# Eight zero writes and four weight loads around the start of the first mixture of experts: two of the writes and all four loads change their place

## The chip, the cores and the metric

The kernel runs on one core of a Trainium2 chip. The metric is the device time of one launch in microseconds (us), as the median of several runs. Below, PE is the matrix engine, DVE the vector engine, ACT the scalar engine, POOL the GpSimd engine and SP the engine that issues most DMAs. POOL also issues DMAs: all indirect ones (gathers and scatters) and some plain ones.

## The reference, cut to what matters

Attention over chunks with a few memory keys gives 1536 rows `x` of 512 numbers. Two mixtures of experts follow, each with 8 experts of two matrices (512x1024 and 1024x512). In the first, every row goes to its two best experts, in the second to its best one as far as the expert has room.

```python
x = attn_out.transpose(0, 2, 1, 3).reshape(B * S, H * D)          # 1536 x 512
# first mixture: for each expert e and each of the two choices k
h = np.maximum(x[mask] @ w1[e], 0.0)
out[mask] += top2_w[mask, k, None] * (h @ w2[e])
# second mixture: the same with the best expert alone and a capacity of 384 rows
```

## The kernel before, in words

**Stages.** The attention runs in 12 steps `t`, one for each tile of 128 rows. `step(t)` works at several tiles at once: scores of tile t+2, `prob` of t+1, `attend` and `normalise` of t (which write the tile `xs`), the transposes of t-1 (`x_tr`, L315) and the gate logits of t-2 (L325, copied by DVE at L326). Routing work for the first four tiles (`route`, L518 on) is fed into DVE's queue between these from step 5 on. Each engine runs its instructions in the order in which the code issues them.

**Rows in DRAM.** `put_x` (L309) writes each tile `xs` to DRAM. There are four buffers for `xs`, so tile t may be written only when the row block of tile t-4 has landed. All puts are issued by SP, in one queue with everything else that SP issues.

**Zeros.** The first mixture adds its results into a DRAM array with an accumulating scatter, so the array must be zero first. It is filled by eight plain DMAs of 520 KB from an SBUF tile `zero` (`blank_rows`, L1388). The table `ZEROS` says how many of them SP issues in which step of the attention; the rest are issued by POOL later, by `meanwhile`.

**Jobs of the first mixture.** Rows are gathered by expert and run as jobs. The first job `V0` takes up to 128 rows of expert 0 from the first four tiles and runs in full precision. The second job, `V8`, is the full job of expert 0: 312 rows, gathered by POOL in three blocks (L775, `ids_l`). PE transposes each block (L783); before the third it runs three filler matmuls (L231, `HEAT`). Then V8's matmuls follow (L835). The other seven experts are ranked by their number of rows and run as S[0] to S[6]; their weights can be loaded only when the ranking is known.

**Weights.** A weight matrix comes in halves of 512 KB (`half`, loads at L749, issued by SP). `raw(h)` loads half h; 8 to 11 are the first four halves of the first ranked expert. ACT and DVE split each into two parts (L769, L770), and a buffer is free again when its half has been split. Halves 8 and 9 use buffers that are free from the start; 10 and 11 must wait for V8's own halves. With `behind`, POOL first writes one element of the buffer, so that the load must wait for what stands ahead in POOL's queue.

**Scatter.** After V0's last matmul its rows are added to the zeroed array by a scatter (L1012), which POOL issues and which waits for all eight zero writes. The gathers of S[0] stand behind it in POOL's queue.

Of the kernel before, what the change touches and what calls it, by code (L numbers as in the profile page):

```python
# [42 lines left out]
RB = 6  # L43
PACE = (1.1, 1.9)
PIECES = {6: (2, 3), 7: (0,), 8: (1,), 9: (4,), 10: (5,)}
ZEROS = {0: 1, 1: 2, 3: 1}
HEAT = (0, 0, 3)
ZT = 2
ZN = 2
# [8 lines left out]
def attention_two_moe_kernel(  # L58
# [7 lines left out]
    nc = tc.nc  # L66
# [120 lines left out]
    xb, st = {}, {}  # L187
# [445 lines left out]
    def ranks(cnt, nv, tag, keep=None):  # L633

        key = rt.tile([128, nv], F32, name="key" + tag)
        nc.vector.scalar_tensor_tensor(key, cnt, 16.0, rev[:, 0:nv], op0=OP.mult, op1=OP.add)
        yield "d"
        if keep is not None:
            nc.vector.tensor_tensor(key, key, keep, op=OP.mult)
            yield "d"  # L640
        cmp_ = rt.tile([128, nv, nv], F32, name="cmp" + tag)
        sq = [128, nv, nv]
        nc.vector.tensor_tensor(cmp_, key[:, None, :].to_broadcast(sq), key[:, :, None].to_broadcast(sq),
                                op=OP.is_gt)
        yield "d"
        rk = rt.tile([128, nv], F32, name="rk" + tag)
        nc.vector.tensor_reduce(rk, cmp_, axis=AX.X, op=OP.add)
        yield "d"
        sel = rt.tile(sq, F32, name="sel" + tag)
        nc.vector.tensor_tensor(sel, iotE[:, 0:nv, None].to_broadcast(sq), rk[:, None, :].to_broadcast(sq),  # L650
                                op=OP.is_equal)
        yield "d"
        od = rt.tile(sq, F32, name="od" + tag)
        nc.vector.tensor_tensor(od, sel, iotE[:, None, 0:nv].to_broadcast(sq), op=OP.mult)
        yield "d"
        odi = rt.tile([128, nv], I32, name="odi" + tag)
        with nc.allow_low_precision(reason="whole numbers"):
            nc.vector.tensor_reduce(odi, od, axis=AX.X, op=OP.add)
        regs = [reg_of(odi[0:1, s:s + 1], nv - 1) for s in range(nv)]
        return sel, lambda s: regs[s]()  # L660
# [25 lines left out]
    def out_ids(ids, raw, sh, pl, tag):  # L686

        t = pl.tile(sh, F32, name="oid" + tag)
        nc.vector.tensor_scalar(t, raw, 0.0, float(2 * N), op0=OP.is_equal, op1=OP.mult)
        o = pl.tile(sh, I32, name="oids" + tag)  # L690
        nc.vector.scalar_tensor_tensor(o, t, float(-NP), ids, op0=OP.add, op1=OP.add)
        return o
# [43 lines left out]
    def half(n, j, wa, wb, r, i, behind=False):  # L736

        h = 2 * n + j
        tag = "A" if h % 4 < 2 else "B"
        raw = wp[tag].tile([128, 2, 512], F32, name="raww", bufs=2)  # L740
        sl = ds(r, 1) if not isinstance(r, int) else slice(r, r + 1)
        if i < 2:
            src = wa[sl].rearrange("e (k p) f -> p (e k) f", p=128)[:, 2 * j:2 * j + 2, 512 * i:512 * i + 512]
        else:
            f = 4 * (i - 2) + 2 * j
            src = wb[sl].rearrange("e (k p) f -> p (e k) f", p=128)[:, f:f + 2, :]
        if behind:
            nc.gpsimd.memset(raw[0:1, 0, 0:1], 0.0)
        nc.sync.dma_start(raw, src)  # L749
        st["half", h] = raw  # L750
# [71 lines left out]
    def run_until(done):  # L822

        while not done():
            bg["next"] = bg["credit"]
            tick(0.0)
# [560 lines left out]
    def blank_rows(z, n, w, eng=nc.sync):  # L1387
        eng.dma_start(z, zero[:, None, 0:w].to_broadcast([128, n, w]))  # L1388
# [19 lines left out]
    V0 = Job("T", 0, caps1[0], True, cols=0)  # L1408
# [4 lines left out]
    n = 0  # L1413
# [54 lines left out]
    zeros = [(zr[:, ZN * i:ZN * i + ZN], ZN, W2) for i in range((N + NP) // (128 * ZN))]  # L1468
    zeros2 = [(zo[:, 4 * i:4 * i + 4], 4, DM) for i in range(N // 512)]
    for t in range(-2, NT):  # L1470
# [4 lines left out]
        if t == ZT:  # L1475
            blank_rows(x_d[0:NP].rearrange("(t p) c -> p t c", p=128), 4, W1)
        for _ in range(ZEROS.get(t, 0)):
            blank_rows(*zeros.pop())
# [44 lines left out]
    def raw(h, behind=False):  # L1523
        n, j = divmod(h, 2)
        s, i = divmod(n + 2 if n >= nh + 2 else n, 4)
        if s < E:
            half(n, j, w1a, w2a, st["regs1"](s - 1) + 1, i)
        elif s == E:
            run_until(lambda: "reg_u" in st)
            half(n, j, w1b, w2b, st["reg_u"](), i)  # L1530
        elif s < 2 * E:
            half(n, j, w1b, w2b, st["regs2"](ORDER2[s - E - 1]), i, behind)


    def h_rank():
        st["sel1"], st["regs1"] = yield from ranks(cnt1[:, 1:E], E - 1, "1")
        for h in range(8, 12):
            raw(h)

    def h_ids():  # L1540
        sel = st["sel1"]
# [30 lines left out]
    def chain():  # L1572
        assert not state["gen"]
        logits(NT - 1)
        yield "lg"
        yield from last
        yield from h_rank()
        yield "ranked"
        for i in range(len(BT)):
            yield from enter(i)  # L1580
        yield "d"
        h_open()
        yield from h_ids()
        yield "z"
        yield from h_rest()
# [197 lines left out]
    def hook(job, u, f):  # L1783
        hooks.setdefault((at[job], u), []).append(f)
# [17 lines left out]
    V0.turns = [2.5, 3, 3]  # L1802

    def meanwhile():
        while zeros:
            blank_rows(*zeros.pop(), nc.gpsimd)
        while next(bg["gen"]) != "ranked":
            pass
        bg["next"] = bg["ready"] = bg["credit"]

    hook(V0, 1.5, meanwhile)
    assert S[4].kind == "M" and S[5].kind == "M"
    S[4].late = overflow_done
    U0.late = drain
# [15 lines left out]
    for job in jobs[1:-1]:  # L1830
        n = job.n0
# [69 lines left out]
```

## Time and profile before

| | |
|---|---|
| time, median of 3 runs | 613.57 us (613.55 to 613.66) |
| profiled execution | 613.34 us, of which 611.6 us from the first to the last instruction |
| PE busy | 587.5 us (96%) |
| DVE, ACT, POOL busy | 371.2 us (61%), 300.0 us (49%), 169.4 us (28%) |
| granted PE clock, mean | 0.99 |
| DMA | 112.12 MB, 183 GB/s over the span |

PE is busy nearly all the time, so what can move the total is PE's idle time and the stretches in which its clock is granted at half. A row of the timeline gives start, duration, engine, line, operation, the tile written and the tiles read, and in brackets the idle time of the engine before it and what ended that. Rows of neighbouring equal instructions are merged (x4). The clock is 1.00 at 2.4 GHz and 0.50 at 1.2 GHz. DMA share is the mean busy share of the core's DMA engines.

### The profile page before, as it was taken

To read this page: it belongs to the slowest core of one execution; us is meant where nothing else is said; L and a number is where in the kernel's file an instruction comes from. 1 tells how busy PE (TensorE), PEld (TensorE's weight loads), DVE (VectorE), ACT (ScalarE), POOL (GpSimd) and SP (SyncE) were. 2 spreads that over 40 slices of the span, in tenths; PEclk is the share of its full clock that TensorE was granted. 3 is DMA by queue.
4 is the path that set the end of the run, shared out by engine and by line. 5 is a ranking of instruction groups with operands and counts; after the bars stand their busy time and mean duration, and the time that the engine had idled before them with its cause. 6 is when DMAs were issued, how large, how long until landed. Compare 5 with 4: busy or idle time off the path is not lost. (4 is left out here: it accounts for less than half of the span.)

```text
span 611.6 us, 12271 instructions
## 1 busy us (share of the span) xinstructions
PE 587.5 (96%) x4539; PEld 522.4 (85%) x4539; DVE 371.2 (61%) x997; ACT 300.0 (49%) x633; POOL 169.4 (28%) x243
## 2 busy tenths in 40 slices
PE   7789999899999999999999999999999999999996
PEld 4678774788999999999999898998978978869984
DVE  8575857577755555555555447364468657457672
ACT  4365444335644445445445445344417557456563
POOL 8885004102612312214112140202351121210202
PEclk9899899899999999999999999999999999999999
DMA  9977863536864855756536665545365676975751
GB/s 245 289 131 268 279 190 81 185 87 207 236 230 139 223 161 142 224 156 141 177 90 150 174 143 156 125 125 156 39 206 177 234 238 203 394 274 178 250 187 41
DMA packets 76426, 112.12 MB, mean 183 GB/s; under 512 B 28225, under 2 KB 28225, under 8 KB 76360
## 3 DMA queue, kind: packets, MB, share of 16 engines
q1 hardware_dynamic: 66936, 86.86, 45.1%
q0 software_dynamic: 9424, 24.41, 16.9%
q8 instruction: 38, 0.62, 0.4%
q14 instruction: 28, 0.23, 0.1%
HBM read 88.90 MB, written 22.07 MB: 181 GB/s over the span
## 5 line engine op out<-in xcount | busy, mean ns | idle before, releaser
L770 DVE TENSOR_TENSOR wlo<-raww,whi 128x512 fp32r<-128x512 f32 x226 | 150.2, 688 | 38.5 <-ACT whi L769 32.3
L769 ACT ACTIVATE whi<-raww 128x512 fp32r<-128x512 f32 x228 | 135.6, 623 | 5.3 <-SPq L1340 2.1
L847 DVE SCALAR_TENSOR_TENSOR hl<-psA,hh 128x256 fp32r<-128x256 f32 (+7 forms) x104 | 53.3, 513 | 76.1 <-ACT hh L846 72.4
L846 ACT ACTIVATE hh<-psA 128x256 fp32r<-128x256 f32 (+7 forms) x104 | 47.3, 455 | 100.7 <-PE psA L835 93.3
L835 PE MATMUL psA<-xh,wlo 128*128 128x256 f32 (+7 forms) x416 | 85.5, 327 | 1.8 <-issue 0.7
L835 PE MATMUL psA<-xl,whi 128*128 128x256 f32 (+7 forms) x416 | 82.6, 321 | 0.0
L835 PE MATMUL psA<-xh,whi 128*128 128x256 f32 (+7 forms) x416 | 82.6, 321 | 0.0
L1012 POOL DMA_INDIRECT x_rows<-yr,ids x25 | 39.2, 1569 | 124.7 <-ACT whi L769 85.6
L835 PEld LDWEIGHTS psA<-xh,wlo 128*128 128x128 f32 x416 | 66.9, 190 | 4.1 <-DVE hl L847 0.8
L835 PEld LDWEIGHTS psA<-xl,whi 128*128 128x128 f32 x416 | 68.8, 190 | 0.4
L835 PEld LDWEIGHTS psA<-xh,whi 128*128 128x128 f32 x416 | 68.6, 189 | 0.3
L775 POOL DMA_INDIRECT xg<-x_rows,ids x37 | 37.9, 1025 | 109.0 <-DVE gs L1052 37.6
L835 PE MATMUL psC<-wlo,hh 128*128 128x512 f32 (+1 forms) x184 | 52.6, 405 | 0.0
L835 PE MATMUL psC<-whi,hh 128*128 128x512 f32 (+1 forms) x184 | 50.7, 395 | 0.0
L835 PE MATMUL psC<-whi,hl 128*128 128x512 f32 (+1 forms) x184 | 50.5, 394 | 0.0
L787 DVE TENSOR_TENSOR xl<-psB,xh 128x512 fp32r<-128x512 f32 (+4 forms) x33 | 21.1, 640 | 38.1 <-ACT xh L786 35.2
L835 PEld LDWEIGHTS psC<-whi,hh 128*128 128x128 f32 (+1 forms) x184 | 34.0, 186 | 8.3
L835 PEld LDWEIGHTS psC<-whi,hl 128*128 128x128 f32 (+1 forms) x184 | 34.1, 186 | 8.0
L835 PE MATMUL psA<-hh,wlo 128*128 128x312 f32 (+4 forms) x160 | 36.9, 351 | 0.8 <-DVE hl L847 0.5
L786 ACT ACTIVATE xh<-psB 128x512 fp32r<-128x512 f32 (+4 forms) x33 | 18.4, 557 | 38.8 <-PE psB L783 36.2
L835 PEld LDWEIGHTS psC<-wlo,hh 128*128 128x128 f32 (+1 forms) x184 | 32.0, 186 | 5.4
L1019 POOL DMA_INDIRECT out_dram<-yr,oids x12 | 12.0, 1002 | 87.8 <-ACT yr L990 49.2
(366 smaller groups left out, 933.8 us busy)
## 6 DMA issues: line engine op xcount, KB each, us to landing
raww<-in_moe_w_dram SPq DMA_DIRECT2D x114, 512.0 KB
raw<-in_k_dram SPq DMA_DIRECT2D x6, 512.0 KB
raw<-in_q_dram SPq DMA_DIRECT2D x6, 512.0 KB
x_rows<-xs SPq DMA_DIRECT2D x12, 256.0 KB
out_dram<-zero SPq DMA_DIRECT2D x3, 1024.0 KB
v<-in_v_dram SPq DMA_DIRECT2D x10, 256.0 KB
x_rows<-zero SPq DMA_DIRECT2D x4, 520.0 KB
x_rows<-zero POOLq DMA_DIRECT2D x4, 520.0 KB
```

The lines of the kernel that those rows point to most:

```text
L769: nc.scalar.activation(hi[:, c], raw, AF.Copy)
L770: (eng or nc.vector).tensor_tensor(lo[:, c], raw, hi[:, c], op=OP.subtract)
L775: return nc.gpsimd.indirect_dma_start(out=xg, out_offset=None, in_=src, in_offset=bass.IndirectOffsetOnAxis(ap=ids_ap, axis=0))
L786: nc.scalar.activation(xh[:, :, o], pv[:, :, 0:n], AF.Copy)
L787: low = lambda: nc.vector.tensor_tensor(xl[:, :, o], pv[:, :, 0:n], xh[:, :, o], op=OP.subtract)
L835: nc.tensor.matmul(ps, w[a], x[b], start=first and i == 0, stop=last and i == n - 1)
L846: nc.scalar.activation(hh[:, f, 0:C], ps[:, 0:C], AF.Relu)
L847: nc.vector.scalar_tensor_tensor(hl[:, f, 0:C], ps[:, 0:C], 0.0, hh[:, f, 0:C], op0=OP.max, op1=OP.subtract)
L1012: wr = nc.gpsimd.indirect_dma_start(out=x2_d, out_offset=off, in_=yr[:n], in_offset=None, compute_op=OP.add)
L1019: wr = nc.gpsimd.indirect_dma_start(out=out, out_offset=off, in_=yr[:n, 0:DM], in_offset=None, bounds_check=N - 1, oob_is_err=False)
```

## The change

The table `ZEROS` loses two writes: SP issues one in step 0 and one in step 1, where it issued one, two, and one more in step 3. The remaining six go to POOL, where four were. `h_rank` no longer issues the loads of halves 8 to 11. A new hook, `weights8`, at the end of V0, issues the zero writes and then the four loads, halves 8 and 9 with `behind`.

```diff
-ZEROS = {0: 1, 1: 2, 3: 1}
+ZEROS = {0: 1, 1: 1}
...
-            half(n, j, w1a, w2a, st["regs1"](s - 1) + 1, i)
+            half(n, j, w1a, w2a, st["regs1"](s - 1) + 1, i, behind)
...
         st["sel1"], st["regs1"] = yield from ranks(cnt1[:, 1:E], E - 1, "1")
-        for h in range(8, 12):
-            raw(h)
...
     def meanwhile():
-        while zeros:
-            blank_rows(*zeros.pop(), nc.gpsimd)
         while next(bg["gen"]) != "ranked":
             pass
...
+    def weights8():
+        while zeros:
+            blank_rows(*zeros.pop(), nc.gpsimd)
+        for h in range(8, 12):
+            raw(h, h < 10)
+
     hook(V0, 1.5, meanwhile)
+    hook(V0, 3, weights8)
```

The order on PE, DVE and ACT stays the same. On POOL, before, from the routing results of the last eight tiles (`gt`) to the gathers of S[0] (`ids_2201`):

```order
L515 TENSOR_TENSOR gt<-gt 128x72
L775 DMA xg<-x_rows,ids_l 128x521 x3
L1388 DMA x_rows<-zero 128x2x520 x4
L1010 MEMSET spacer 1x1
L1012 DMA x_rows<-yr,ids_e 2048x520
L775 DMA xg<-x_rows,ids_2201 128x521 x4
```

The same place in the changed kernel:

```order
L515 TENSOR_TENSOR gt<-gt 128x72
L775 DMA xg<-x_rows,ids_l 128x521 x3
L1388 DMA x_rows<-zero 128x2x520 x6
L748 MEMSET raww 1x1 x2
L1010 MEMSET spacer 1x1
L1012 DMA x_rows<-yr,ids_e 2048x520
L775 DMA xg<-x_rows,ids_2203 128x521 x4
```

The zero writes stood behind V8's three gathers already; there are two more of them, and the two one-element writes that halves 8 and 9 wait for stand behind them.

On SP, before, in the attention from step 0 to step 4 (`memv` rows are small copies of memory values, the 128x4x521 write is another zero fill, of the rows array):

```order
L1388 DMA x_rows<-zero 128x2x520
L309 DMA x_rows<-xs 128x512
L141 DMA v_76<-memv 8x2x520 x2
L1388 DMA x_rows<-zero 128x2x520 x2
L309 DMA x_rows<-xs 128x512
L141 DMA v_76<-memv 8x2x520 x2
L1388 DMA x_rows<-zero 128x4x521
L309 DMA x_rows<-xs 128x512
L141 DMA v_76<-memv 8x2x520 x2
L1388 DMA x_rows<-zero 128x2x520
L309 DMA x_rows<-xs 128x512
```

The same stretch in the changed kernel:

```order
L1388 DMA x_rows<-zero 128x2x520
L309 DMA x_rows<-xs 128x512
L141 DMA v_76<-memv 8x2x520 x2
L1388 DMA x_rows<-zero 128x2x520
L309 DMA x_rows<-xs 128x512
L141 DMA v_76<-memv 8x2x520 x2
L1388 DMA x_rows<-zero 128x4x521
L309 DMA x_rows<-xs 128x512
L141 DMA v_76<-memv 8x2x520 x2
L309 DMA x_rows<-xs 128x512
```

One zero write fewer stands ahead of the second, third and fourth put, and the one just ahead of the fourth put is gone too.

On SP, before, the loads of the first halves of the ranked expert, with what each waits for (`DMAHW` is the landing of an earlier DMA of SP's):

```order
L668 TENSOR_LOAD odi_1870 [waits DVE_49]
L668 ISA x2
L749 ISA
L749 DMA raww<-in_moe_w_dram 128x2x512 [waits DMAHW7_49]
L749 ISA
L749 DMA raww<-in_moe_w_dram 128x2x512 [waits DMAHW0_49]
```

The same loads in the changed kernel:

```order
L668 TENSOR_LOAD odi_1864 [waits DVE_49]
L668 ISA x2
L749 ISA
L749 DMA raww<-in_moe_w_dram 128x2x512 [waits DMAHW5_49,Pool_49]
L749 ISA
L749 DMA raww<-in_moe_w_dram 128x2x512 [waits DMAHW6_49,Pool_49]
```

Both loads now wait for POOL; nothing else on SP has changed its order there.

## Rows read from the trace of the kernel before

**Rows 1.** PE's waits, 86 to 250 us: waiting, for whom, total us, times, longest
```profile
PE psD L783 <- DMA xg<-x_rows,ids_l: 2.8, 1, 2.8
```

**Rows 2.** PE's waits, 250 to 612 us
```profile
PE psB L783 <- DMA xg<-x_rows,ids_ul: 1.0, 1, 1.0
```

**Rows 3.** PE's timeline, around the start of V8
```profile
103.31 0.60 PE L783 MATMUL psD<-ident,xg 128*128 128x128 f32 x4
...
105.91 0.81 PE L231 MATMUL psD<-warmer 128*128 128x512 bf16 x3
109.49 0.63 PE L783 MATMUL psD<-ident,xg 128*128 128x128 f32 x4 [2.77 <-DMA xg<-x_rows,ids_l]
110.56 0.95 PE L835 MATMUL psA<-xh,wlo 128*128 128x312 f32 x4 [0.45 <-ACT xh L786]
```

**Rows 4.** POOL's timeline, the same place and on
```profile
99.65 1.21 POOL L775 DMA_INDIRECT xg<-x_rows,ids_l  x1 [3.89 <-DVE wlo L770]
...
102.42 0.95 POOL L775 DMA_INDIRECT xg<-x_rows,ids_l  x1 [0.30 <-issue]
103.37 2.95 POOL L1388 DMA_DIRECT2D x_rows<-zero  x4
...
119.78 1.70 POOL L1012 DMA_INDIRECT x_rows<-yr,ids_e  x1 [13.39 <-DVE yr L1006]
135.95 1.39 POOL L775 DMA_INDIRECT xg<-x_rows,ids  x1 [14.47 <-issue]
```

**Rows 5.** SP's timeline, 101 to 104 us
```profile
102.31 1.03 SPq L749 DMA_DIRECT2D raww<-in_moe_w_dram  x2
```

**Rows 6.** Half-us windows: stretch, length, PE busy, granted clock, DMA share, GB/s
```profile
105.50:106.00 0.50, 0.50 (x6) 1.00 0.65 94
...
109.00:109.50 0.50, 0.01 (x1) 1.00 1.03 419
...
111.00:111.50 0.50, 0.50 (x4) 0.63 1.06 399
...
114.50:115.00 0.50, 0.50 (x5) 0.95 0.28 83
```

**Rows 7.** DVE's timeline in the attention
```profile
57.66 0.42 DVE L303 TENSOR_TENSOR xs<-psC,rs 128x256 f32<-128x256 f32 x1 [2.30 <-DMA x_rows<-xs]
...
66.11 0.17 DVE L326 COPY lgs<-psD 128x18 f32<-128x18 f32 x1
```

**Rows 8.** SP's timeline in the attention
```profile
49.92 0.97 SPq L1388 DMA_DIRECT2D x_rows<-zero  x2
51.01 0.98 SPq L309 DMA_DIRECT2D x_rows<-xs  x1
```

**Rows 9.** Windows: stretch, length, DVE busy, granted clock, DMA share, GB/s
```profile
52.00:54.00 2.00, 1.03 (x3) 1.00 1.01 372
...
57.66:66.28 8.62, 8.17 (x42) 1.00 0.86 261
```

**Rows 10.** PE's timeline in the attention
```profile
58.30 1.36 PE L288 MATMUL psC<-v,ex 64*32 64x65 f32 x64 [0.20 <-PE psB L272]
...
62.81 1.11 PE L288 MATMUL psC<-v,ex 64*32 64x65 f32 x64
...
66.33 0.18 PE L554 MATMUL psD<-msk,tri 128*128 128x36 bf16 x1 [1.02 <-DVE lgs L326]
```

**Rows 11.** Half-us windows in the attention, columns as in group 6
```profile
66.50:67.00 0.50, 0.50 (x16) 0.76 0.29 20
...
70.00:70.50 0.50, 0.50 (x5) 0.83 1.06 402
```

**Rows 12.** A half-us window at another short idle time, columns as in group 6
```profile
48.00:48.50 0.50, 0.15 (x4) 1.00 1.02 391
```

**Rows 13.** ACT's timeline: a weight split in the attention, the first use of half 8
```profile
69.32 0.63 ACT L769 ACTIVATE whi<-wlo 128x512 fp32r<-128x512 f32 x1 [1.92 <-DMA wlo<-in_moe_w_dram]
...
134.46 1.14 ACT L769 ACTIVATE whi<-raww 128x512 fp32r<-128x512 f32 x2
```

## The prediction

> **What bounds the kernel now.** I read PE's waits first, since PE is busy for 96% of the span. From 86 us on PE loses little: one wait of 2.77 us, when V8 starts, for the third block of gathered rows [rows 1, 3], and later none longer than 1.0 us [rows 2]. So a gain must come from PE's idle time and from its clock, and there are two places where both occur.
>
> *Place A, the start of V8.* PE ends its filler matmuls at 105.91 + 0.81 = 106.72 and transposes the third block only at 109.49; V8's matmuls begin at 110.56 [rows 3]. The half-us windows show the granted clock at 0.63 from 111.00, so it fell to half (1.2 GHz) at about 111.13, and 0.95 from 114.50, so it came back at about 114.55 [rows 6]: 3.42 us at half clock, after the idle time.
>
> *Place B, the attention near 66 us.* DVE waits 2.30 us, to 57.66, for a put to land, because tile 5 takes over the buffer of tile 1 [rows 7]. From there to the end of the copy of the gate logits at 66.28 DVE is busy 8.17 of 8.62 us [rows 7, 9]: routing work has been put into its queue, and it cannot catch up. PE feels it twice: `attend` at 58.30 starts 0.20 late and takes 1.36 instead of 1.11, and the first routing matmul waits 1.02 us, to 66.33, for that copy [rows 10]. The clock falls right after, at about 66.76 (0.76 in the window from 66.50), and is back at about 70.17 (0.83 from 70.00): 3.41 us at half [rows 11].
>
> **The change part by part.**
>
> *The put of tile 1 lands earlier (B).* It is issued at 51.01, behind three zero writes, two of them just ahead at 49.92 [rows 8]. One of the two goes. A write is 520 KB, 0.53 MB; at the 372 GB/s of the stretch from 52 to 54 us [rows 9], in which the DMA engines are full, that is 1.43 us. If the put lands that much earlier, DVE starts the block at 56.23 instead of 57.66 (its inputs are there at 55.36, where its idle time begins). Then `attend` at 58.30 loses its 0.20 + 0.25 = 0.45 us. The copy at 66.11 could come 1.43 earlier; PE's logits, which it needs, come 0.45 earlier, so PE's wait shrinks to the copy (0.17) and a hand-over, some 0.25 instead of 1.02: 0.77 us. And if the idle time is that short, the clock should stay up: an idle time at 48 us, in which PE did only 0.15 us of work in half a us, left it at 1.00 [rows 12]. That gives back half of 3.41, 1.70 us. Sum 0.45 + 0.77 + 1.70 = 2.92. ACT stands against the last part: it waits 1.92 us, to 69.32, for a weight piece, and that DMA moves little with the compute [rows 13]. Bounds 0 and 2.9; I take **2.6**, near the upper one, since PE, not ACT, is without a gap after 66.33.
>
> *The zero write of step 3* and its issue on SP go as well; the puts behind leave earlier, and no row of PE or DVE waits for them. Nothing.
>
> *The third gather lands earlier (A).* POOL issues the gathers at 99.65, 101.17 and 102.42 [rows 4]. PE could use the first block at 103.31 without a wait [rows 3], so that one took at most 3.66 us. The third took 109.49 - 102.42 = 7.07. What differs: SP issues halves 8 and 9, together 1.05 MB, from 102.31 on [rows 5], and the rate in the window at 105.50 is 94 GB/s with PE's gather still out, against 419 at 109.00 [rows 6]. In the changed kernel these loads wait for two writes that POOL does after six zero writes. At 2.95 / 4 = 0.74 us each POOL is through at 103.37 + 6 x 0.74 = 107.8, so the loads start 5.5 us later, behind the gathers. The third gather then lands at about 102.42 + 3.66 = 106.1, before the filler ends at 106.72. PE's wait of 2.77 goes, and with it the fall of the clock: half of 3.42, 1.71. The 0.45 us for ACT's part of the block stays [rows 3]. Sum 4.48; bounds 0 (the gather is held by the zero writes behind it) and 4.5. I take **4.4** and leave a tenth of a us for DVE, which splits weights there.
>
> *What the rule of the Trainium skill would make of A.* The Trainium skill ("DMA: Bandwidth & Descriptors", section "Queues, rings and completion order") says that each DMA engine goes round the queues packet by packet. By that rule two loads on SP's queue can at most halve the gather's share, and it would speak against this part: the rival C below. The 7.07 us of the third gather do not agree with an even share alone.
>
> *Halves 8 and 9 start later.* They are first used at 134.46 [rows 13], in the changed kernel some 4.4 us earlier by A (B moves both ends alike): 130.1. From 107.8 six zero writes (3.2 MB) and the two halves need 4.25 MB / 0.4 MB per us = 10.6 us at the rate of 399 to 419 GB/s [rows 6], so they are there by about 118.4: nothing, the cover is 11 us. Halves 10 and 11 still wait for the split of V8's own halves.
>
> *Two more zero writes on POOL* are 1.5 us of issue in a hole of 13.39 us before V0's scatter [rows 4]. That scatter must wait for all zeros, at the latest until 118.4, where its rows are now ready about 4.4 earlier than 119.78; it may start up to 3 us late, with the gathers of S[0] behind it on POOL, due at 135.95 - 4.4 = 131.5 [rows 4]. 11 us are left: nothing.
>
> *Two fewer issues on SP*, 0.97 / 2 = 0.49 us each [rows 8]: off the path.
>
> **Sum.** 4.4 + 2.6 = 7.0 us. The profiled execution took 613.34 us, 1.74 of it outside the span of 611.6; 613.34 - 7.0 = 606.3. The median, 613.57, is 0.23 above the profiled one, so the forecast is **606.6**. The stages after V8 follow PE's own order and have no wait over 1.0 us [rows 1, 2], so I see nothing that takes the 7.0 back.
>
> **The rivals.**
>
> *A alone.* The put lands earlier, but its last packets, or the chain from the scores through DVE, keep PE's wait near 66 us and the clock falls still. For it: an idle time of 1.02 us is not much longer than the one at 48 us [rows 10, 12], so a small rest may do. Against it: 1.43 us is more than the whole wait. B then gives 0 to 1.2 (its two idle terms): 613.57 - 4.4 - 0.6 = 608.6, from 608.0 to 609.2.
>
> *C: the gather stays late.* What holds the third gather is not the loads but the zero writes, which POOL issues right behind it without a gap, at 103.37 [rows 4], and which stay there. The even share of the rule above points this way. Against it: the zeros stand behind the gather in the same queue, and they run at 419 GB/s once it has landed. B alone: 613.57 - 2.6 = 611.0.
>
> *Nothing happens.* Neither the put nor the gather was held by what is moved: 613.4, within 0.2%.
>
> *Slower: the zeros hold S[0].* Six zero writes and two halves are 4.25 MB on top of the gathers, and the scatter waits for the last zero, with S[0]'s gathers behind it. At the 94 GB/s of the window at 105.50 [rows 6] they would take 45 us, to about 151; S[0]'s gathers would come 1.7 us after that, 21 us late, and the time would be 606.6 + 21 = 628. It starts to cost when the zeros land after 131.5 - 1.7 = 129.8, that is below 4.25 / 23.7 = 0.18 MB per us, and the kernel is slower than before below about 0.13. Against it: the same kind of writes ran at 399 to 419 GB/s.
>
> **How the numbers follow.** Forecast 0.59, A alone 0.21, C 0.08, nothing 0.07, slower 0.05. With A between 4.0 and 4.5 and B between 1.5 and 2.9 the forecast's own range is 606.2 to 608.1. Below that, ACT's wait of 1.92 us could shrink by half as the pieces leave SP earlier, 0.9 more: 605.3. A alone reaches to 609.8 if A is 3.8 and B nothing. The range 605.3 to 609.8 leaves out C, nothing and slower, 0.20. A change of 0.2%, 1.2 us, is about what a measurement of this kernel can tell from none; faster by more than that: 0.59 + 0.21 + 0.08 = 0.88; within it 0.07; slower 0.05.
>
> **What would show it.** A is right if PE transposes the third block at about 106.7 (less what B gives) without a wait, the loads of halves 8 and 9 start about 5.5 us after the place where they start now, and no window between 107 and 115 us has a clock under 1.00. B is right if DVE's wait for the put is under 1 us, the first routing matmul waits less than 0.5 us and the clock stays at 1.00 to the end of the attention. A gather that still takes over 6 us with the loads behind it refutes A and leaves C; a clock that falls near 66 us though DVE's wait is gone refutes my reading of B. If PE waits for half 8, for the scatter or for S[0]'s gathers, the cover that I counted is gone.

## The result, and the profile after

The changed kernel took **607.95 us** (median of 4 runs, 607.68 to 608.63) against 613.62 us for the kernel before on the same chip (4 runs, 613.55 to 616.39). The ratio is 0.9898 (95% interval 0.987 to 0.9927). The profiled execution took 607.77 us, 606.0 of it in the span, and the mean granted clock was 0.998 where it had been 0.99. The forecast was 606.6 with a range of 605.3 to 609.8: the time is inside the range, the direction and the two places are right, and the gain is 5.67 us where 7.0 were predicted.

*Place A.* PE's timeline at the start of V8, to be set beside [rows 3] (start, duration, engine, line, operation, tiles, and idle time with what ended it):

```profile
103.06 0.60 PE L783 MATMUL psD<-ident,xg 128*128 128x128 f32 x4
103.49 0.81 PE L231 MATMUL psD<-warmer 128*128 128x512 bf16 x3
104.36 0.66 PE L783 MATMUL psD<-ident,xg 128*128 128x128 f32 x4
105.47 0.84 PE L835 MATMUL psA<-xh,wlo 128*128 128x312 f32 x4 [0.45 <-ACT xh L786]
106.15 0.73 PE L835 MATMUL psA<-xl,whi 128*128 128x312 f32 x4
```

The transposes of the third block follow the filler without a wait. The half-us windows at V8 and near 66 us, to be set beside [rows 6] and [rows 11] (here with every engine's busy time, then granted clock, DMA share and GB/s), have full clock:

```profile
104.50:105.00 0.50, 0.50 (x4) 0.28 (x3) 0.50 (x1) 0.00 (x0) 0.50 (x2) 1.00 0.99 391
...
111.00:111.50 0.50, 0.50 (x7) 0.50 (x6) 0.50 (x1) 0.15 (x1) 0.00 (x0) 1.00 1.10 360
...
66.50:67.00 0.50, 0.50 (x3) 0.20 (x2) 0.50 (x1) 0.48 (x1) 0.42 (x3) 1.00 1.18 426
```

POOL's timeline, the counterpart of [rows 4]:

```profile
100.01 0.95 POOL L775 DMA_INDIRECT xg<-x_rows,ids_l  x1 [0.30 <-issue]
100.95 4.36 POOL L1388 DMA_DIRECT2D x_rows<-zero  x6
105.29 0.12 POOL L748 MEMSET raww<- 1x1 f32 x2
...
115.70 1.70 POOL L1012 DMA_INDIRECT x_rows<-yr,ids_e  x1 [10.26 <-ACT whi L769]
129.21 1.39 POOL L775 DMA_INDIRECT xg<-x_rows,ids  x1 [11.82 <-issue]
```

From the issue of the third gather to PE it is now 104.36 - 100.01 = 4.35 us at most, and was 7.07. The two loads start behind POOL's one-element writes, in SP's timeline (against [rows 5]):

```profile
105.40 1.88 SPq L749 DMA_DIRECT2D raww<-in_moe_w_dram  x2
```

*Place B.* SP's first zero write, then the one zero write and the put of tile 1 on SP (against [rows 8]), and what DVE and PE make of it (against [rows 7] and [rows 10]), each from that engine's timeline:

```profile
45.16 0.43 SPq L1388 DMA_DIRECT2D x_rows<-zero  x1
...
48.52 0.43 SPq L1388 DMA_DIRECT2D x_rows<-zero  x1
49.06 0.40 SPq L309 DMA_DIRECT2D x_rows<-xs  x1
...
55.45 0.42 DVE L303 TENSOR_TENSOR xs<-psC,rs 128x256 f32<-128x256 f32 x1
...
58.08 1.11 PE L288 MATMUL psC<-v,ex 64*32 64x65 f32 x64
...
65.11 0.18 PE L554 MATMUL psD<-msk,tri 128*128 128x36 bf16 x1 [0.27 <-DVE lgs L326]
```

DVE does not wait for the put, `attend` takes 1.11 us, and the wait of 1.02 us is 0.27.

**Where the 5.6 us of the span come from.** PE runs the same 4539 matmuls in the same order, so each can be set against itself; the lead of the changed kernel grows and shrinks along the run:

| place | start before | start after | lead | change |
|---|---|---|---|---|
| `attend`, second matmul pair near 58 us | 58.65 | 58.22 | 0.43 | +0.4 |
| first routing matmul (L554) | 66.33 | 65.11 | 1.22 | +0.8 |
| behind the old fall of the clock (L272) | 70.12 | 67.35 | 2.77 | +1.6 |
| last transpose of `xs` (L315) | 85.78 | 83.37 | 2.41 | -0.4 |
| third block of V8 (L783) | 109.49 | 104.36 | 5.12 | +2.7 |
| behind the old second fall (L835) | 114.64 | 108.00 | 6.63 | +1.5 |
| V8, before its second matrix (L835) | 122.98 | 116.24 | 6.74 | +0.1 |
| S[0]'s second block (L783) | 146.26 | 139.83 | 6.43 | -0.3 |
| block of `ids_ul` (L783) | 453.88 | 447.64 | 6.24 | -0.2 |
| last block of rows (L783) | 602.79 | 596.92 | 5.86 | -0.4 |

So A gave 4.2 and B 2.8, the 7.0 of the forecast. Then 1.3 us go away again at four places, and 0.2 more behind the last block. Three of the four in PE's timeline after, with what ended each:

```profile
83.37 0.27 PE L315 MATMUL psD<-ident,xs 128*128 128x128 f32 x1 [0.26 <-issue]
...
139.83 0.63 PE L783 MATMUL psB<-ident,xg 128*128 128x128 f32 x4 [0.48 <-DMA xg<-x_rows,ids]
...
596.92 0.63 PE L783 MATMUL psB<-ident,xg 128*128 128x128 f32 x4 [0.21 <-DMA xg<-x_rows,own_i]
```

The first has no cause in the profile. The other two are gathers, which POOL issued just as early relative to PE as before, and which came 0.2 to 0.4 us later.

### The profile page after: what moved, and what is told of

The parts are those of the page before. It is cut to its first block, busy times and chain, and to the rows that moved or that the text cites. A ratio compares the mean times of both kernels' runs of the same rounds, so it can differ in the third digit from the quotient of the medians.

```text
span 606.0 us, 12277 instructions
## 1 busy us (share of the span) xinstructions
PE 583.7 (96%) x4539; PEld 519.5 (86%) x4539; DVE 370.9 (61%) x997; ACT 300.2 (50%) x633; POOL 170.5 (28%) x247
## 5 line engine op out<-in xcount | busy, mean ns | idle before, releaser
L835 PE MATMUL psA<-xh,wlo 128*128 128x256 f32 (+7 forms) x416 | 84.9, 325 | 1.7 <-issue 0.7
L835 PE MATMUL psA<-xh,whi 128*128 128x256 f32 (+7 forms) x416 | 82.1, 319 | 0.0
L835 PE MATMUL psA<-xl,whi 128*128 128x256 f32 (+7 forms) x416 | 82.0, 319 | 0.0
L835 PEld LDWEIGHTS psA<-xh,wlo 128*128 128x128 f32 x416 | 66.4, 188 | 4.0 <-issue 1.2
L835 PEld LDWEIGHTS psA<-xl,whi 128*128 128x128 f32 x416 | 68.2, 188 | 0.3
L835 PEld LDWEIGHTS psA<-xh,whi 128*128 128x128 f32 x416 | 68.1, 188 | 0.3
L835 PE MATMUL psC<-wlo,hh 128*128 128x512 f32 (+1 forms) x184 | 52.6, 406 | 0.0
L835 PE MATMUL psC<-whi,hh 128*128 128x512 f32 (+1 forms) x184 | 50.7, 395 | 0.0
L835 PE MATMUL psC<-whi,hl 128*128 128x512 f32 (+1 forms) x184 | 50.4, 394 | 0.0
L835 PEld LDWEIGHTS psC<-whi,hh 128*128 128x128 f32 (+1 forms) x184 | 34.0, 186 | 8.3
L835 PEld LDWEIGHTS psC<-whi,hl 128*128 128x128 f32 (+1 forms) x184 | 34.1, 186 | 8.0
L835 PE MATMUL psA<-hh,wlo 128*128 128x312 f32 (+4 forms) x160 | 36.9, 351 | 0.8 <-DVE hl L847 0.5
L835 PEld LDWEIGHTS psC<-wlo,hh 128*128 128x128 f32 (+1 forms) x184 | 32.0, 186 | 5.5
```

Of the source, the lines that this page charges most:

```text
L835: nc.tensor.matmul(ps, w[a], x[b], start=first and i == 0, stop=last and i == n - 1)
```

## The experiments

My theory was that the two halves of the change act at two places and add up: the loads of halves 8 and 9 hold the third gather (A), the zero write ahead of the put of tile 1 holds the put (B). Rival C was that the zero writes behind the gather hold it. The experiments ran on three chips, on each of which executions of one kernel spread over 4 to 10 us (the kernel before: 609.2 to 619.2 us). So I give the ratio to the kernel before on the same chip with its interval (it is not the quotient of the two medians and differs from it by up to 0.25%), and read each place in the profile of one execution. That execution can lie far from the median: it is the slowest of its kernel's in the first run of the loads alone (615.01 us), in step 1 alone (615.05) and in the late zero writes (617.36), and the fastest in the dose (607.81). So a profile shows that something happens, not how often.

**Zero writes alone, and loads alone.**

```diff
-ZEROS = {0: 1, 1: 2, 3: 1}
+ZEROS = {0: 1, 1: 1}
```

> The kernel before with the new table of zero writes alone (one in step 0, one in step 1, six on POOL); halves 8 to 11 are loaded where they were. My theory (the two halves of the change act at two places and add up): place B alone, so the put of tile 1 lands about 1.4 us earlier, DVE's wait of 2.30 us and PE's wait of 1.02 us near 66 us go, the clock stays at 1.00 there; in the changed kernel that was worth 2.4 us at 85 us. The third gather of V8 still takes about 7 us, PE waits 2.8 us for it and the clock falls to half behind it: 613.6 - 2.4 = 611.2 us (610.7 to 611.7). Rival (one place is enough: a start of V8 that comes earlier meets other traffic, or the gain of the attention is taken back at V8): within 0.5 us of 613.6, or below 610. Rival C (zero writes behind the gather hold it; here they are six instead of four): PE's wait at V8 grows, up to 4.3 us, and the time is 611.5 to 613.

Measured: 613.61 us, ratio 0.9993 (0.9965 to 1.0022): no gain that can be told from none, where 2.4 us were expected. PE's timeline:

```profile
66.18 0.18 PE L554 MATMUL psD<-msk,tri 128*128 128x36 bf16 x1 [0.27 <-DVE lgs L326]
...
109.34 0.63 PE L783 MATMUL psD<-ident,xg 128*128 128x128 f32 x4 [3.59 <-DMA xg<-x_rows,ids_l]
```

Place B is free of the wait here, with full clock from 65 to 70 us; V8 waits 3.59 us, 0.8 more than before, and the gather takes 109.34 - 101.48 = 7.86 us. The other half alone:

```diff
-        for h in range(8, 12):
-            raw(h)
...
+    def weights8():
+        while zeros:
+            blank_rows(*zeros.pop(), nc.gpsimd)
+        for h in range(8, 12):
+            raw(h, h < 10)
```

> The kernel before with the loads of halves 8 and 9 behind POOL's zero writes alone (four of them on POOL, as before, with the old table). My theory: place A alone. The third gather takes about 3.6 us, PE transposes its block without a wait, no half-us window between 107 and 116 us has a clock under 1.00; near 66 us the wait of 1.0 us and the fall of the clock stay. In the changed kernel place A was worth 4.2 to 4.3 us: 613.6 - 4.25 = 609.4 us (608.9 to 609.9). Rival C (the zero writes hold the gather): 613.6, gather still 7 us. Rival (the clock's fall at V8 is an after-effect of the fall near 66 us): 610.9 to 611.1, the wait gone but the clock at half for 3.4 us behind V8's start.

Measured: 609.51 us, ratio 0.9926 (0.9901 to 0.9951), the 4 us expected. The profile, of the slowest of its nine executions, shows the two places apart. DVE's and PE's timelines:

```profile
59.26 0.42 DVE L303 TENSOR_TENSOR xs<-psC,rs 128x256 f32<-128x256 f32 x1 [2.19 <-DMA x_rows<-xs]
...
68.83 0.18 PE L554 MATMUL psD<-msk,tri 128*128 128x36 bf16 x1 [1.24 <-DVE lgs L326]
...
109.41 0.66 PE L783 MATMUL psD<-ident,xg 128*128 128x128 f32 x4
110.51 0.84 PE L835 MATMUL psA<-xh,wlo 128*128 128x312 f32 x4 [0.45 <-ACT xh L786]
```

Its windows of 1 us, columns as above:

```profile
70.00:71.00 1.00, 0.90 (x18) 0.84 (x16) 0.07 (x2) 0.00 (x0) 0.71 (x3) 0.50 0.67 205
...
112.00:113.00 1.00, 1.00 (x9) 1.00 (x8) 0.01 (x1) 0.47 (x2) 0.00 (x0) 1.00 1.05 333
```

Place B is there whole (wait of DVE, wait of PE, half clock), place A is gone whole. The fall of the clock at V8 is thus no after-effect of the one near 66 us.

**Step 1 alone**, with step 3's write kept, in the kernel before:

```diff
-ZEROS = {0: 1, 1: 2, 3: 1}
+ZEROS = {0: 1, 1: 1, 3: 1}
```

> The kernel before with one zero write fewer in step 1 of the attention and the one of step 3 kept (five on POOL); loads where they were. My theory: the write ahead of the put of tile 1 makes all of place B, the one of step 3 nothing: the same as the run with both moved, 611.2 us (610.7 to 611.7), DVE's wait at tile 5 gone. Rival (step 3's write counts as well, by the puts behind it or the traffic of that stretch): at least 0.4 us slower than that run, and PE's waits near 66 us are only partly gone.

Measured: 612.84 us where 611.2 were expected, ratio 0.996 (0.9927 to 0.9993). DVE starts its block without a wait, PE's wait is 0.27 (L554 at 66.39): step 3's write makes no wait in this execution, as predicted. One execution does not show that the write of step 1 makes it alone, since the wait is missing in some executions with the whole old table too, as is seen below. V8's gather took 109.30 - 101.02 = 8.28 us here. Against the run before the intervals overlap, so nothing is read from their difference.

**Zero writes alone, again**, on another chip:

> The table of zero writes alone once more, since executions of one kernel spread over 9 us where it ran first. Place by place, from the first run: near 66 us the wait of 1.0 us is 0.3 and the clock stays up (2.4 to 2.8 us gained there), the third gather takes 7 to 8 us with loads and six zero writes beside it, so PE's wait at V8 is 2.8 to 3.6 us and the clock falls behind it (0 to 0.8 lost there). My theory: 613.6 - 2.4 + 0.4 = 611.6 us (610.8 to 612.2). Rival (place B is not there in most executions of the kernel before, so that its removal gives little): within 0.7 us of the kernel before.

Measured: 612.34 us against 613.19, ratio 0.9998 (0.9966 to 1.003). Place B is free of the wait again (L554 waits 0.27, clock 1.00), PE waits 2.56 us for the third gather (6.89 us from its issue). So in both runs the rival holds: removing the writes alone gives little. A possible reason is seen further below.

**Loads early, zero writes late.** POOL's four writes wait for V8's third block:

```diff
+            if self is V8 and blk == 2:
+                nc.gpsimd.tensor_copy(spacer, st["x"][0][0:1, 0, 256:257])
+                while zeros:
+                    blank_rows(*zeros.pop(), nc.gpsimd)
```

> The kernel before, in which POOL's four zero writes wait until the third block of V8 has been transposed and copied (a one-element copy on POOL reads that block ahead of them); halves 8 and 9 are loaded early, as before. So the gather has the loads beside it and no zero writes. My theory (the loads hold the gather): the third gather still takes about 7 us, PE waits 2.5 to 2.8 us, the clock falls: 613.6 us (613.2 to 614.0). Rival C (the zero writes that POOL issues right behind it hold it): the gather takes 3.6 us, wait and fall of the clock go: 609.4 us. Both together: in between, with a gather of 4.5 to 6 us.

Measured: 612.94 us, ratio 0.9989 (0.996 to 1.0017). POOL's and PE's timelines:

```profile
101.25 0.95 POOL L775 DMA_INDIRECT xg<-x_rows,ids_l  x1 [0.30 <-issue]
108.77 0.18 POOL L1102 COPY spacer<-xh 1x1 f32<-1x1 f32 x1 [6.57 <-ACT xh L786]
...
107.69 0.63 PE L783 MATMUL psD<-ident,xg 128*128 128x128 f32 x4 [2.14 <-DMA xg<-x_rows,ids_l]
```

The clock behind that wait, in a window of 1 us:

```profile
109.00:110.00 1.00, 1.00 (x5) 1.00 (x6) 0.98 (x5) 0.00 (x0) 1.00 (x2) 0.50 0.00 0
```

With the loads beside it and no zero write in flight the gather still takes 6.44 us, PE waits 2.14 us and the clock falls. Rival C falls: the loads hold the gather. With zero writes behind it as well it took 6.89 to 8.28 us in the runs here, so they may add some tenths of a us; one execution each cannot size that.

**Filler in the kernel before**, to part the idle time from the clock:

```diff
-HEAT = (0, 0, 3)
+HEAT = (0, 0, 14)
```

> The kernel before with 14 filler matmuls instead of 3 ahead of V8's third block; nothing else moves. Eleven more at 0.22 us are 2.4 us, which end at about 109.1, before the gather lands. My theory (the clock falls because PE has nothing to do for 2.8 us): PE's wait shrinks to about 0.3 us, the clock stays at 1.00 behind it, and the half of the fall is gained while the idle time is only filled: 613.6 - 1.6 = 612.0 us (611.6 to 612.4). Rival (the clock falls there for another reason, the f32 matmuls that begin at 110.56): the clock is at 0.50 from about 111 to 114.5 us as before, 613.6 us.

Measured: 612.11 us against 613.19, ratio 0.9996 (0.9965 to 1.0027). PE's timeline:

```profile
104.21 3.19 PE L231 MATMUL psD<-warmer 128*128 128x512 bf16 x13
108.11 0.63 PE L783 MATMUL psD<-ident,xg 128*128 128x128 f32 x4 [0.72 <-DMA xg<-x_rows,ids_l]
```

The clock right behind, in a half-us window:

```profile
110.50:111.00 0.50, 0.50 (x6) 0.50 (x4) 0.00 (x0) 0.00 (x0) 0.00 (x0) 1.00 1.04 391
```

With PE kept busy the clock stays up in the very place where it fell, before the same f32 matmuls. In this execution PE gains 1.4 us on the kernel before between 75 and 115 us (lead 1.50, then 2.91), which is the half of the fall. The whole time cannot show it within its interval.

**No filler in the changed kernel**, to see when the gather lands:

```diff
-HEAT = (0, 0, 3)
+HEAT = (0, 0, 0)
```

> The changed kernel without the three filler matmuls ahead of V8's third block. It shows when the gather lands, which the filler hides in the changed kernel. My theory (a gather alone takes 3.6 to 3.7 us from its issue at 100.01): PE, which comes to the block at 103.5 instead of 104.3, waits 0.1 to 0.4 us for it, the clock stays: 607.95 - 0.5 = 607.5 us (607.1 to 607.9). Rival (the gather had only just landed at 104.3, so nothing is left between it and PE): PE waits 0.8 us, 607.95, or 609.5 if the clock falls too. Rival (it landed much earlier): no wait, 607.2.

Measured: 608.68 us where 607.5 were expected, ratio 0.9933 (0.99 to 0.9966). POOL's and PE's timelines:

```profile
101.71 0.95 POOL L775 DMA_INDIRECT xg<-x_rows,ids_l  x1 [0.30 <-issue]
...
105.93 0.63 PE L783 MATMUL psD<-ident,xg 128*128 128x128 f32 x4 [0.56 <-DMA xg<-x_rows,ids_l]
107.00 0.84 PE L835 MATMUL psA<-xh,wlo 128*128 128x312 f32 x4 [0.45 <-ACT xh L786]
```

PE waits 0.56 us, more than I expected, and the groups behind it keep their 0.73 us, so the clock stays. A gather without loads beside it takes 105.93 - 101.71 = 4.22 us from issue to PE. The filler's end hides it in the changed kernel with about 0.1 us to spare (104.23 against 104.36), not with the 0.6 of the prediction.

**All eight zero writes on POOL**, in the changed kernel:

```diff
-ZEROS = {0: 1, 1: 1}
+ZEROS = {}
```

> The changed kernel with all eight zero writes on POOL, none on SP. Two more writes are 1.5 us of POOL and 1.04 MB more that must land before V0's scatter, 2.6 us later (it started at 115.7 in the changed kernel, so 118.3 here). My theory (the scatter and the gathers of S[0] behind it have 10 us of cover, and the puts have no wait left to lose): 607.95 us (607.5 to 608.4), S[0]'s gathers where they were. Rival (the writes of steps 0 and 1 still hold something in the attention): faster, up to 1 us. Rival (S[0] is held): slower by over 0.5 us, with a wait of PE at 138 to 140 us.

Measured: 608.93 us, ratio 0.9956 (0.9927 to 0.9985); the interval overlaps that of the run before it. POOL's timeline:

```profile
99.93 5.76 POOL L1388 DMA_DIRECT2D x_rows<-zero  x8
...
117.65 2.19 POOL L1012 DMA_INDIRECT x_rows<-yr,ids_e  x1 [11.81 <-ACT hh L846]
128.19 1.38 POOL L775 DMA_INDIRECT xg<-x_rows,ids  x1 [8.35 <-DVE wlo L770]
```

V0's scatter starts 117.65 - 103.33 = 14.3 us behind V8's third block (11.3 in the changed kernel), and S[0]'s gathers 24.9 us behind it, as in the changed kernel: the cover is real, and no cost of the two more writes shows there.

**The changed kernel, the loads alone, and a dose of zero writes, on one chip.** The dose is the changed kernel with four writes ahead of the put of tile 1:

```diff
-ZEROS = {0: 1, 1: 1}
+ZEROS = {0: 1, 1: 3}
```

> The changed kernel itself, beside the three below on one chip, so that their times can be set against it. Theory so far: place A is worth 4.2 us wherever it runs (gather 4.3 us or less, clock at 1.00); place B is worth 2.8 us in an execution in which the put of tile 1 lands late under the old table, and nothing in one where it does not. 613.6 - 4.2 - (0 to 2.8) = 606.6 to 609.4 us, 4.5 to 6 us under the kernel before on the same chip. Rival (A and B overlap): less than 4 us under it.

> The loads behind the zero writes with the old table, beside the changed kernel on the same chip: the difference of the two is what the new table gives with place A mended. Theory: 2.4 to 2.8 us in executions with DVE's wait for the put, 0 in others, so the median is 0.5 to 2.5 us above that of the changed kernel, and the profile shows either a wait of DVE of about 2 us at tile 5 with PE's wait of over 1 us near 66 us and a fall of the clock, or none of the three. Rival (the table gives nothing): the same as the changed kernel within 0.3 us.

> The changed kernel with three zero writes in step 1 instead of one (four on POOL): four writes now stand ahead of the put of tile 1, three just ahead of it. Theory: the put lands 2 x 1.43 = 2.9 us later than in the changed kernel and 1.43 later than with the old table, so DVE's wait at tile 5 is about 2.3 + 1.4 = 3.7 us (or 1.4 where the old table gives none), PE waits 1 to 3 us more between 58 and 67 us and the clock falls: 1.4 to 2 us above the run with the old table, some 3 to 4.5 us above the changed kernel. Rival (the wait is not made by the writes ahead of the put): no more than the run with the old table.

Measured, against 613.41 for the kernel before there:

| | us | ratio (95%) | DVE's wait at tile 5 | PE's wait at L554 | clock near 66 us |
|---|---|---|---|---|---|
| changed kernel | 608.48 | 0.9921 (0.9898 to 0.9944) | 0.44 | 0.27 | 1.00 |
| loads alone | 610.13 | 0.9958 (0.9932 to 0.9984) | 0.48 | 0.69 | 1.00 |
| dose | 610.64 | 0.9956 (0.9933 to 0.9978) | 0.64 | 0.27 | 1.00 |

DVE's and PE's timelines of the loads alone, then of the dose:

```profile
55.50 0.42 DVE L303 TENSOR_TENSOR xs<-psC,rs 128x256 f32<-128x256 f32 x1 [0.48 <-DMA x_rows<-xs]
...
65.14 0.18 PE L554 MATMUL psD<-msk,tri 128*128 128x36 bf16 x1 [0.69 <-DVE lgs L326]
```

```profile
56.48 0.42 DVE L303 TENSOR_TENSOR xs<-psC,rs 128x256 f32<-128x256 f32 x1 [0.64 <-DMA x_rows<-xs]
...
65.81 0.18 PE L554 MATMUL psD<-msk,tri 128*128 128x36 bf16 x1 [0.27 <-DVE lgs L326]
```

Place A is mended in all three. In the dose's profile, with one write *more* ahead of the put than in the kernel before, DVE waits 0.64 us and not 3.7, and the clock stays: my price of 1.43 us a write does not hold in this execution. But it is the fastest of the dose's twelve, 2.8 us under their median, so it says little of the others.

In the times the writes ahead of the put do show: eight of the twelve executions of the changed kernel took under 609 us, two of the loads alone and two of the dose. The medians order as expected (the loads alone 1.65 us above the changed kernel), but the intervals of the two touch, and the profiles do not put the difference at place B. The first routing matmul starts at 65.14 in the loads alone and at 65.32 in the changed kernel beside it. The loads alone fall behind later, by a clock at half from 88.0 to 91.4 us and by a wait of 1.94 us for the gather of `ids_ul`, which is 0.92 in the changed kernel.

So what made the wait of 2.30 us? Two things go with it. The first is how early SP issues the put. The table sets the issue (the start of SP's row) against the moment at which DVE needs the buffer (where its wait begins), in us:

| execution | put issued | DVE needs it | between | DVE starts | after the issue |
|---|---|---|---|---|---|
| kernel before | 51.01 | 55.36 | 4.35 | 57.66 | 6.65 |
| loads alone, first run | 52.98 | 57.07 | 4.09 | 59.26 | 6.28 |
| loads alone, second run | 49.58 | 55.02 | 5.44 | 55.50 | 5.92 |
| dose | 50.38 | 55.84 | 5.46 | 56.48 | 6.10 |
| loads early, zero writes late | 50.16 | 55.69 | 5.53 | 55.91 | 5.75 |

SP's timeline of the kernel before (its first zero write), of the first run of the loads alone, then of the second:

```profile
46.20 0.43 SPq L1388 DMA_DIRECT2D x_rows<-zero  x1
```

```profile
52.98 2.60 SPq L309 DMA_DIRECT2D x_rows<-xs  x1
```

```profile
49.58 1.13 SPq L309 DMA_DIRECT2D x_rows<-xs  x1
```

In the two executions with a wait of over 2 us SP issued the put over 1 us closer to DVE's need than in the others. With the same table of writes, the kernel before with more filler had 6.44 us between the two (49.43 and 55.87) and no wait. Against the second run of the loads alone, the later issue makes 1.09 of the 1.82 us by which the kernel before waits longer, and 1.35 of the 1.71 us in the first run; the later landing makes the rest. What held SP is not shown.

The second is the put's last packets. In the kernel before 120 of the put's 128 packets have ended by 55.5 us, when DVE would need them, but the last eight end only between 56.0 and 57.0. The first run of the loads alone has the same tail (120 by 57.5, eight more from 58.0 to 59.0). And both have a packet of 16 KB of the queue that the profile calls instruction (by that name, code for an engine), which starts while the zero writes fill every DMA engine. The DMA view of the kernel before, 51 to 53 us (queue, kind: packets, MB, share of 16 engines):

```profile
q8 instruction: 1, 0.02, 5.8%
```

The same row of the loads alone, first run, 53 to 55 us:

```profile
q8 instruction: 1, 0.02, 5.3%
```

That is 5.8% of 16 x 2 us = 1.86 us, and 1.70 us. In the dose the same row has 3.0%, 0.96 us. The two executions with the long packet in that stretch are the two with a wait of over 2 us (2.30 and 2.19) and the only two of fourteen in which the clock fell near 66 us. In the changed kernel's first profile the packet took 0.95 us and DVE did not wait. This fits a put whose last share is queued behind the code on one engine. But it is a coincidence of fourteen profiles, not shown by an experiment, and by the table it can make only the smaller part of what the two wait longer than the second run. The changed kernel's second profile has such a tail too (120 packets by 54.1 us, the last eight from 54.7 to 55.3) and a wait of 0.44 us.

**Filler where the longest wait is left** (four filler matmuls ahead of the block of `ids_ul`, in the changed kernel):

```diff
+            if self.hot:
+                warm(self.hot)
...
+    UL.hot = 4
```

> The changed kernel with four filler matmuls on PE ahead of the first block of the job whose gather reads ids_ul, where PE waited 1.0 to 4.0 us in the profiles so far, the longest wait left, with the clock at half behind the waits of 1.9 and 4.0 us. The filler is 0.9 us, less than the shortest wait, so it costs nothing. Theory: an execution with a wait of 1 us is unchanged, one with 1.5 to 3 us saves up to 1.5 us because the clock stays: the median is 0 to 0.8 us below that of the changed kernel. Rival (the gather lands when it lands and the clock does not fall in most executions): the same within 0.3 us.

Measured: 609.52 us, ratio 0.9947 (0.9922 to 0.9972), not better than the changed kernel beside it. PE's timeline:

```profile
447.58 0.66 PE L783 MATMUL psB<-ident,xg 128*128 128x128 f32 x4 [1.02 <-DMA xg<-x_rows,ids_ul]
```

In this execution the gather came later and the wait behind the filler was still 1.02 us, and the clock had nothing to lose. No ratio here is below those of the changed kernel (0.9898 and 0.9921).

## Why the prediction was right, and where it was not

- **Place A, 4.4 predicted, 4.2 measured.** The wait of 2.77 went whole (+2.7), the clock gave 1.5 where half of 3.42 is 1.71. Right in the mechanism too: loads alone mend it, and rival C fell with the zero writes held back. One term was mis-sized. I took 3.66 us for a gather alone, from the first one; the third takes 4.22, and the cover by the filler is thinner than it looked.
- **The even share.** The prediction set the 7.07 us against the rule of the Trainium skill ("DMA: Bandwidth & Descriptors", section "Queues, rings and completion order") that a DMA engine goes round its queues packet by packet, and said that an even share alone does not agree. Measured against 4.22 for the gather alone, 7.07 is 1.7 times as long, and 6.44 with loads and no zero writes is 1.5 times. Both are below twice, so the trace is consistent with the rule, and the step was wrong; even against the prediction's own 3.66, 7.07 is 1.9 times. The rule does not make rival C out of it: the loads alone are enough for the wait.
- **Place B, 2.6 predicted, 2.8 measured there, in part by luck.** The three terms came as worked out (0.4, 0.8 and 1.6, for 0.45, 0.77 and 1.70). The price under them was mis-sized: "If the put lands that much earlier" by one write's 1.43 us. In the changed kernel's profile the put's last packet ends at 52.23 and not at 56.94, 4.7 us earlier. Part of that was there before any write was removed: SP's first zero write, which the change does not touch, starts 10.29 us before DVE's need and not 9.16 (45.16 and 55.45 after, 46.20 and 55.36 before). The prediction's profile was one of the two of fourteen with a wait of over 2 us; in the eight profiles with at most two zero writes ahead of that put DVE never waited for it more than 0.44 us, but of the six with three or more only two waited long. So the sum of 7.0 priced an event that many executions do not have, and on another chip the change gave 4.9 us (608.48 against 613.41). What B is worth on average, and by what, stays open: the zero writes alone were 0.4 to 0.9 us ahead of the kernel before, within their intervals, and the loads alone 1.65 us behind the changed kernel, with no loss at place B in the profile.
- **What costs nothing.** Right, as far as the profiles show: step 3's write, the later halves 8 and 9 (no wait for their splits in PE's waits), two more zero writes, the scatter up to 3 us late. V0's scatter started 2.7 us later than its lead of 6.74 would put it, and S[0]'s gathers had the full lead.
- **"I see nothing that takes the 7.0 back."** This step failed: 1.3 us went at four places, 0.2 to 0.4 us at each, which the prediction left out since no wait there was over 1.0. The gathers of S[0] and of the last rows land within tenths of a us of PE's need, that of `ids_ul` 1 us behind it, and they shift from one execution to the next, so this part of the miss may be chance. It is about the whole difference between 606.6 and 607.95.

## What to carry to other kernels

A wait for a small transfer is cured by holding back the large transfer beside it, if that one has slack; make it wait behind the small one's issue, and check that its first use is still covered. Cost a wait together with the clock behind it: of the 7.0 us that the two places gave, 3.1 were the clock. Before you price a wait by bytes divided by rate, look in more than one execution at whether the wait is there, how early the transfer was issued, and which of its packets are late.

## What was not expected of the hardware

- **Packets of the queue called instruction share the DMA engines with data.** One of 16 KB took 1.86 and 1.70 us in the two executions above, with a DMA share of 0.97 meanwhile, and 0.95 us in the second run of the loads alone, with a DMA share of 0.99. So full engines alone do not make it long. Whether it delays a transfer is not shown.
- **The length of an idle time does not decide alone whether PE's clock falls.** It fell behind 1.02 us [rows 10, 11] and behind 1.93 us at the block of `ids_ul` in the first run of the loads alone (clock 0.50 from 455 to 458 us), but not behind 2.83 us at the same block in the second run of the zero writes alone. PE's timeline of that run, and then a window of it:

```profile
454.37 0.63 PE L783 MATMUL psB<-ident,xg 128*128 128x128 f32 x4 [2.83 <-DMA xg<-x_rows,ids_ul]
```

```profile
455.00:456.00 1.00, 1.00 (x6) 0.78 (x5) 0.34 (x1) 0.60 (x1) 0.83 (x1) 1.00 1.08 414
```

  In the second run of the loads alone it fell behind a wait of only 0.36 us, and not behind the same wait at the same place in the changed kernel beside it. PE's timeline of the first with a window of it, then PE's timeline of the second:

```profile
86.57 1.04 PE L325 MATMUL psD<-wg,xt 128*128 128x18 f32 x8 [0.36 <-DVE lgs L326]
87.45 5.38 PE L909 MATMUL psA<-whi,xf 128*128 128x512 f32 x8
...
88.00:89.00 1.00, 1.00 (x3) 0.48 (x2) 0.45 (x2) 0.42 (x2) 0.00 (x0) 0.50 0.76 293
```

```profile
87.29 3.68 PE L909 MATMUL psA<-whi,xf 128*128 128x512 f32 x8
```

- **The same gather** (`ids_ul`) made PE wait from 0.92 to 4.01 us in the thirteen profiles without that filler, with the same instructions around it; from POOL's issue to PE it took 3.6 to 6.8 us. It is the largest wait left, and what moves it stays open.
